# A transformer block on one core: WQ loaded ahead of the second quarter of x, normalisation on ACT, low parts on GpSimd, and one visit of six units per projection

## The chip, the core and the metric

The kernel runs on one core of a Trainium2 chip. A core has five engines that run side by side, each through its own list of instructions in order: TensorE (PE, matrix multiplication, with its weight loads listed as PEld), VectorE (DVE), ScalarE (ACT), GpSimd (POOL) and SyncE (SP), which here issues all DMA transfers. They wait for each other through semaphores only. The metric is the device time of one execution in microseconds. Before the change it is 1258.13 us (median of three runs, 1256.53 to 1259.32).

## The reference

One block of a transformer, with S = 2048 rows of width D = 448, H = 16 heads of width 28 that share one key and one value projection, and a gated feed-forward part of width 1792, all in float32:

```python
def _A_ref(x, wq, wk, wv, wo):
    q = (x @ wq).reshape(B, S, H, Dh).transpose(0, 2, 1, 3)
    k = x @ wk
    v = x @ wv
    scores = jnp.einsum("bhqd,bkd->bhqk", q, k) * (Dh ** -0.5)
    p = softmax(scores, axis=-1)
    o = jnp.einsum("bhqk,bkd->bhqd", p, v)
    return o.transpose(0, 2, 1, 3).reshape(B, S, H * Dh) @ wo
...
h = x + _A_ref(layernorm(x), wq, wk, wv, wo)
return h + (silu(layernorm(h) @ w1) * (layernorm(h) @ w3)) @ w2
```

## The kernel before

**Numbers in two parts.** Most products are made of two rounded halves: a value is split into a high part (an ACT copy into the type float32r) and a low part (the value less its high part), and a product is high by high, low by high and high by low. `mm_D` (L120 to L131) does that for the width 448: eleven matmuls into one PSUM bank, and after the sixth of them it calls `between()` if one is given.

**Quarters.** The 2048 rows are four quarters t = 0 to 3 of 512 columns. For each quarter the program, in the part this change touches, does five things. `stats(t)` takes mean and variance of the four row blocks on DVE (L155, L156), and the inverse root on GpSimd (L161). `norm(t)` makes the four normalised blocks `xn` (L166, DVE) and copies 64 columns of each to its end (L168, GpSimd). `tr(t)` transposes them on PE in four groups c (L179), each into a bank; ACT takes the high part `xh` (L180), and the low part `xl` is a subtraction, on DVE straight from the bank (L187, L189), or, with `spare`, on GpSimd from a copy `rb` that ACT makes of the bank (L184). Of `rb` there are two buffers. `kv(t)` is one `mm_D` for keys and values: ACT writes the high part of the keys (L422), DVE the low part (L423), ACT the values (L425), and then SP copies the 64 rows of the keys to the other 64 partitions (L426) and, when that copy has landed, puts four rows of ones in (L427). `q(t, g)` is one `mm_D` for four heads, taken out by ACT (L446; the first one, and later ones by `build_qs`, go on to the tile QS, by eight DMAs each, L213).

**Units.** Softmax needs the maximum of each row of scores before the exponentials. A `Unit` is one matmul of 128 queries by one quarter kt of the keys (L231, on 64 of the 128 rows of the array) and one maximum over its 512 columns on DVE (L236); `both` is two of them, for the two halves of the array. In the first stage 40 `both`, 80 units, are worked off: 64 of the first group of heads (kt = 0 first, then 1, 2, 3), the maximum over them (L248), and 16 of the second group, with the transposed maxima sent to QS between them (L253 to L267). The list is `first`, and `pairs(n)` takes n `both` from its front. They are mixed with the projections: called as `between` inside an `mm_D` two `both` are taken, and one more by a `pairs(1)` between two projections. They begin when two quarters are through and the third is transposed.

**Banks.** There are seven PSUM banks, given out in the order in which they were released. Every unit, projection and transposed group takes one. So a unit waits for whatever last used its bank: a maximum on DVE, an ACT copy, a DVE copy.

**After that** the main stage begins: for each of 16 groups of heads and 16 key blocks, matmuls (L280), exponentials (L286) and the product with the values (L293), with the units of later groups between them, and then the feed-forward part. Neither is changed, apart from two small GpSimd instructions in each later call of `ln_rstd`.

The order is written out by hand in the program. The loads at the start stand on SP's list in the order first quarter of x, wk, wv, second quarter of x, wq, third, fourth.

Of the kernel before, what the change touches and what calls it, by code (L numbers as in the profile page):

```python
# [16 lines left out]
P = 128  # L17
# [18 lines left out]
def block_kernel(  # L36
# [112 lines left out]
    def ln_stats(t, n):  # L149
        if n == 0:  # L150
            LN[t] = (ln_pool.tile([P, NQ, 6], F32, name="st"),
                     ln_pool.tile([P, NQ, 2], F32, name="mv"),
                     ln_pool.tile([P, NQ], F32, name="rs"), {})
        st, mv, _, _ = LN[t]
        ve.bn_stats(st[:, n], X[t][:, n])  # L155
        ve.bn_aggr(mv[:, n], st[:, n])  # L156

    def ln_rstd(t, n0=0, n1=NQ):
        _, mv, rs, _ = LN[t]
        ve.tensor_scalar(rs[:, n0:n1], mv[:, n0:n1, 1], EPS, None, op0=ALU.add)  # L160
        ge.tensor_tensor(rs[:, n0:n1], rs[:, n0:n1], pexp[:, n0:n1], op=ALU.pow)  # L161

    def ln_norm(t, n):
        _, mv, rs, xns = LN[t]
        xn = xns[n] = ln_pool.tile([P, 512], F32, name="xn", bufs=4)
        ve.tensor_scalar(xn[:, :D], X[t][:, n], mv[:, n, 0:1], rs[:, n : n + 1],  # L166
                         op0=ALU.subtract, op1=ALU.mult)
# [196 lines left out]
    with tc.tile_pool(name="start", bufs=1) as sp:  # L364
# [10 lines left out]
        for m0, w in ((0, wk), (64, wv)):  # L375
            load_w(wkv_r[:, :, m0 : m0 + DH], w)
        sy.dma_start(X[1], xv[1])
        load_w(wq_r, wq)
# [31 lines left out]
        def norm(t):  # L410
            for n in range(NQ):
                ln_norm(t, n)

        def tr(t, *cs):
            for c in cs or range(4):
                ln_tr(t, c)

        def kv(t, between=None):
# [9 lines left out]
            done(ps)  # L428
            return vt

# [24 lines left out]
        def pairs(n=2):  # L455
            while n > 0 and first:
                fn, *args = first.pop(0)
# [275 lines left out]
```

## Time and profile before

| what | us |
|---|---|
| median of three runs | 1258.13 |
| the profiled execution, its own time | 1257.51 |
| its span in the trace | 1255.7 |
| first stage, to the first matmul of L280 | 99.07 |
| main stage, to the first matmul of the feed-forward part | 715.73 |
| feed-forward part | 440.90 |
| PE busy over the span | 1235.7 |
| DVE busy over the span | 860.8 |
| ACT busy over the span | 660.9 |
| POOL busy over the span | 324.3 |

The 1.8 us between the span and the profiled execution's time lie around the traced span. A row of the timeline has the start, the time until the end of the last of its instructions, the engine, the line, the operation, what it writes and reads, the count, and in brackets how long the engine had been idle and what released it. A row of the windows has a window's bounds and length and then, for each engine, busy time and (in brackets) instructions, the granted clock of PE as a share of full speed, and the DMA engines' share and rate. A row of the groups has the count, the busy time, the mean duration of one and the idle time ahead of it.

### The profile page before, as it was taken

How to read it: one execution, taken by the hardware profiler on the slowest of the kernel's cores; microseconds unless marked ns; L12 is line 12 of the kernel's file. 1: busy time of each engine (PE TensorE's matmuls, PEld its weight loads, DVE VectorE, ACT ScalarE, POOL GpSimd, SP SyncE). 2: the span in 40 equal slices, each digit the busy share in tenths (PEclk: the TensorE clock that was granted, in tenths of full speed). 3: DMA queues.
4: the chain of work that ended last, by engine and by line, in shares of the span. 5: the costliest groups of instructions: out<-in, count | busy, mean ns of one | idle time of the engine just before them, and what ended most of it. 6: DMA issues, size and time to landing. Idle time of an engine off the chain costs nothing.

```text
span 1255.7 us, 19960 instructions
## 1 busy us (share of the span) xinstructions
PE 1235.7 (98%) x7596; PEld 768.0 (61%) x7596; DVE 860.8 (69%) x1480; ACT 660.9 (53%) x1255; POOL 324.3 (26%) x240
## 2 busy tenths in 40 slices
PE   6999999999999999999999999999999999999998
PEld 4655444444544444544445543488888888888887
DVE  7998999999898999899998894033333334333333
ACT  3316878887688887688886687921111111211111
POOL 3201011101112101111110110344555445455551
PEclk9999999999999999999999999999999999999999
DMA  6220113110103110112110110023000000000000
GB/s 188 62 45 2 36 32 77 44 25 21 44 2 77 44 40 6 43 24 56 43 45 2 43 28 17 10 79 111 1 30 1 1 1 30 1 1 31 1 1 30
DMA packets 37960, 43.08 MB, mean 34 GB/s; under 512 B 12056, under 2 KB 30680, under 8 KB 37864
## 3 DMA queue, kind: packets, MB, share of 16 engines
q1 hardware_dynamic: 37864, 41.81, 12.8%
q8 instruction: 60, 0.98, 0.3%
q14 instruction: 36, 0.29, 0.1%
HBM read 20.25 MB, written 3.80 MB: 19 GB/s over the span
## 4 chain that ended last, share of the span: by engine, by line
PE 91%; DVE 6%; issue 1%; DMA 1%; POOL 0%; SPq 0%; ACT 0%; POOLq 0%
PE pa L127 23%; PE pb L280 21%; PE po L293 19%; PE pb L641 11%; PE pa L231 9%; DVE mx L236 5%; PE pb L127 4%; PE pa L330 3%; PE pb L179 1%; DMA qs<-mr 0%; PE pb L253 0%; DVE xn L166 0%; DVE nm L248 0%; SPq L267 0%; DMA X<-in_A_x_dram 0%
## 5 line engine op out<-in xcount | busy, mean ns | idle before, releaser
L236 DVE TENSOR_REDUCE mx<-pa 128x1 f32<-128x512 f32 x1024 | 635.9, 682 | 36.3 <-PE pa L231 14.8
L286 ACT ACTIVATE pt<-pb 128x512 f32<-128x512 f32 x1024 | 533.9, 601 | 153.9 <-PE pb L280 118.1
L280 PE MATMUL pb<-qs,KS 64*128 64x512 f32 x2048 | 358.2, 403 | 2.0 <-DMA qs<-mr 2.0
L280 PEld LDWEIGHTS pb<-qs,KS 64*128 64x128 f32 x2048 | 227.5, 185 | 159.8 <-DVE mx L236 80.5
L231 PE MATMUL pa<-KS,qs 64*128 64x512 f32 x1024 | 291.7, 441 | 0.9 <-ACT vt L425 0.9
L293 PE MATMUL po<-pt,VA 128*32 128x512 f32 x2048 | 274.4, 606 | 0.0
L127 PE MATMUL pa<-xh,qs 128*128 128x512 f32 x896 | 235.9, 395 | 0.0
L231 PEld LDWEIGHTS pa<-KS,qs 64*128 64x128 f32 x1024 | 133.7, 184 | 130.8 <-DVE mx L236 86.8
L127 PEld LDWEIGHTS pa<-xh,qs 128*128 128x128 f32 x896 | 167.8, 187 | 38.6 <-issue 0.8
L629 DVE TENSOR_TENSOR pt<-pa,pt 128x512 f32<-128x512 f32 x56 | 38.7, 691 | 222.7 <-PE pa L127 222.7
L641 PE MATMUL pb<-qst,pt 128*128 128x448 f32 x672 | 145.8, 367 | 0.0
L627 ACT ACTIVATE pt<-pa 128x512 f32<-128x512 f32 x56 | 33.5, 598 | 197.6 <-PE pa L127 197.5
L641 PEld LDWEIGHTS pb<-qst,pt 128*128 128x128 f32 x672 | 125.7, 188 | 12.5
L632 ACT ACTIVATE pt<-pt 128x512 fp32r<-128x512 f32 x56 | 35.4, 632 | 152.1 <-DVE pt L629 152.1
L202 POOL TENSOR_TENSOR qst<-QR,qst 128x512 fp32r<-128x512 f32 x15 | 19.3, 1285 | 314.7 <-ACT qst L201 314.7
L127 PE MATMUL pa<-xl,qs 128*128 128x512 f32 x336 | 96.4, 395 | 0.0
L293 PEld LDWEIGHTS po<-pt,VA 128*32 128x32 f32 x2048 | 40.9, 108 | 78.6 <-issue 72.0
L340 POOL TENSOR_TENSOR qs<-QR,qs 128x1024 fp32r<-128x1024 f32 x32 | 76.4, 2388 | 16.2 <-DVE qs L339 16.2
L317 POOL TENSOR_TENSOR OT<-OT,rb 128x512 f32<-128x512 f32 x16 | 20.8, 1298 | 201.3 <-PE pb L280 70.7
L127 PEld LDWEIGHTS pa<-xl,qs 128*128 128x128 f32 x336 | 62.9, 187 | 15.5
L633 DVE TENSOR_TENSOR pt<-pt 128x512 fp32r<-128x512 f32 x56 | 40.8, 728 | 39.1 <-ACT pt L632 39.1
L346 POOL TENSOR_TENSOR qst<-w_wo,qst 128x448 fp32r<-128x448 f32 x24 | 35.3, 1469 | 93.9 <-DVE qst L345 93.9
(80 smaller groups left out, 632.2 us busy)
## 6 DMA issues: line engine op xcount, KB each, us to landing
qs<-qst SPq DMA_DIRECT2D x128, 128.0 KB
rb<-sd SPq DMA_DIRECT2D x64, 64.0 KB
QR<-in_B_w_dram SPq DMA_DIRECT2D x16, 192.0 KB
X<-in_A_x_dram SPq DMA_DIRECT2D x3, 896.0 KB
out_dram<-X SPq DMA_DIRECT2D x3, 896.0 KB
qs<-mr SPq DMA_DIRECT2D x128, 2.0 KB
w<-in_B_w_dram SPq DMA_DIRECT2D x8, 192.0 KB
w_wo<-in_B_w_dram SPq DMA_DIRECT2D x6, 224.0 KB
```

Of the source, the lines that this page charges most:

```text
L127: pe.matmul(ps, lhs[b][:, cb, lsl], rhs[a][:, ca, rsl], start=(k == 0), stop=(k == len(terms) - 1),)
L231: pe.matmul(self.ps, QS[i][r, 2 * self.p, n * P : (n + 1) * P], KS[r, kt * T : (kt + 1) * T], start=True, stop=True)
L236: ve.tensor_reduce(MX[self.i][:, c, self.kt : self.kt + 1], self.ps, axis=AX.X, op=ALU.max)
L280: pe.matmul(self.ps, KS[r, c * P : (c + 1) * P], QS[i][r, 2 * p + k], start=(k == 0), stop=(k == 1))
L286: se.activation(f(PT[i, c, p][:, jj]), self.ps, AF.Exp, bias=0.0, scale=SCALE)
L293: pe.matmul(PO[i][32 * j : 32 * j + 32], VA[:, c], f(PT[i, c, j // 2][:, j % 2]), start=(c == 0), stop=(c == NC - 1))
L330: pe.matmul(ps, OS[a][:, g, n * P : (n + 1) * P], WO[b][:, g], start=(k == 0), stop=(k == 11))
L340: ge.tensor_tensor(wl, W13[k], f(wh), op=ALU.subtract)
L629: ve.tensor_tensor(sg, ps[1], sg, op=ALU.mult)
L632: se.activation(h[:, 0], sg, AF.Copy)
L633: ve.tensor_tensor(h[:, 1], sg, f(h[:, 0]), op=ALU.subtract)
L641: pe.matmul(Y[t][n][:, :D], hid[a][:, n * P : (n + 1) * P], w2s[:, b, :D], start=(k == 0 and m == 0), stop=(k == NF - 1 and m == 2))
```

## The change

WQ goes ahead of the second quarter of x on SP. `norm` of quarters 1 to 3 goes from DVE to ACT, as scale times x plus bias, and for that `ln_rstd` makes a bias `nb` with two GpSimd instructions. The low parts of the transposed quarters 1 to 3 go from DVE to GpSimd, with ACT's second copy `rb`. The order is rewritten: the statistics of the second quarter come after the first `kv`, and the units begin inside the fourth projection of the first quarter. Every unit is taken inside an `mm_D`, three `both` at a time, and `pairs(1)` between projections is gone; since the units begin before all keys are there, `pairs` stops where the next unit's quarter of the keys has not been projected yet.

```diff
     def ln_rstd(t, n0=0, n1=NQ):
...
+        if n1 - n0 == NQ:
+            ge.tensor_tensor(nb, mv[:, :, 0], rs, op=ALU.mult)
+            ge.tensor_scalar(nb, nb, -1.0, None, op0=ALU.mult)
...
+        if act:
+            se.activation(xn[:, :D], X[t][:, n], AF.Identity, bias=nb[:, n : n + 1], scale=rs[:, n : n + 1])
+        else:
+            ve.tensor_scalar(xn[:, :D], X[t][:, n], mv[:, n, 0:1], rs[:, n : n + 1],
+                             op0=ALU.subtract, op1=ALU.mult)
...
+        load_w(wq_r, wq)
         sy.dma_start(X[1], xv[1])
-        load_w(wq_r, wq)
...
         def norm(t):
             for n in range(NQ):
-                ln_norm(t, n)
+                ln_norm(t, n, True)
...
-                ln_tr(t, c)
+                ln_tr(t, c, t > 0)
...
-        def pairs(n=2):
+        def pairs(n=3):
             while n > 0 and first:
-                fn, *args = first.pop(0)
+                fn, *args = first[0]
+                if fn is both and args[3] >= keys[0]:
+                    return
+                first.pop(0)
...
-        tr(0, 0, 1)
-        stats(1, 0)
-        tr(0, 2)
-        stats(1, 1)
-        tr(0, 3)
-        stats(1, 2, 3)
+        tr(0)
         split_wq()
         v0 = kv(0)
+        stats(1, 0, 1, 2, 3)
+        q(0, 0)
         norm(1)
-        q(0, 0)
+        q(0, 1)
+        va(0, v0)
+        stats(2, 0, 1, 2, 3)
         tr(1)
-        stats(2, 0, 1, 2, 3)
-        va(0, v0)
-        q(0, 1)
-        v1 = kv(1)
+        q(0, 2)
         norm(2)
+        q(0, 3, pairs)
+        build_qs(1)
+        v1 = kv(1, pairs)
         stats(3, 0, 1, 2, 3)
-        q(0, 2)
-        q(0, 3)
-        build_qs(1)
         tr(2)
+        q(1, 0, pairs)
         va(1, v1)
-        pairs(1)
+        norm(3)
+        q(1, 1, pairs)
         v2 = kv(2, pairs)
-        pairs(1)
-        norm(3)
-        q(1, 0, pairs)
-        pairs(1)
-        q(1, 1, pairs)
-        pairs(1)
+        q(1, 2, pairs)
         va(2, v2)
-        q(1, 2, pairs)
+        q(1, 3, pairs)
         build_qs(2)
-        pairs(1)
-        q(1, 3, pairs)
         tr(3)
-        pairs(1)
+        q(2, 0, pairs)
         v3 = kv(3, pairs)
         load_wo()
-        for t in (2, 3):
-            for g in range(NG):
-                pairs(1)
-                if (t, g) == (2, 1):
-                    va(3, v3)
-                q(t, g, pairs)
+        for t, g in [(2, 1), (2, 2), (2, 3), (3, 0), (3, 1), (3, 2), (3, 3)]:
+            q(t, g, pairs)
+            if (t, g) == (2, 1):
+                va(3, v3)
         pairs(64)
```

In the changed program the lines of these functions stand a few lines further down: units are L237 and L242, the low part of the keys L429, the low parts on GpSimd L193 and L195, the copies of the keys L432 and L433.

**First place: PE from the third quarter's transposes to the end of `q(1, 0)`, changed program.** `ident` and `xn` are a transpose, `xh`, `xl` and `OS` (which holds WQ here) a projection, `KS` and `qs` a unit; a name in brackets is what the instruction waits for.

```order
L185 MATMUL pb<-ident,xn 128x128 [waits DVE_49,Pool_49]
L185 MATMUL pb<-ident,xn 128x128 [waits Pool_49] x3
L127 MATMUL pb<-xh,OS_95 128x512 [waits DVE_49]
L127 MATMUL pb<-xh,OS_95 128x512 x2
L127 MATMUL pb<-xl,OS_95 128x512 x3
L237 MATMUL pa<-KS,qs 128x512 [waits DVE_49]
L237 MATMUL pa<-KS,qs 128x512 [waits Activation_49]
L237 MATMUL pa<-KS,qs 128x512 [waits PE_49,Activation_49] x2
L237 MATMUL pa<-KS,qs 128x512 [waits DMAHW3_49,PE_49,Activation_49]
L237 MATMUL pa<-KS,qs 128x512 [waits DMAHW2_49,PE_49,Activation_49]
L127 MATMUL pb<-xh,OS_96 128x512 x3
```

The same projection on PE in the program before:

```order
L231 MATMUL pa<-KS,qs 128x512 [waits DVE_49] x2
L127 MATMUL pb<-xh,OS_95 128x512 [waits DVE_49]
L127 MATMUL pb<-xh,OS_95 128x512 x2
L127 MATMUL pb<-xl,OS_95 128x512 x3
L231 MATMUL pa<-KS,qs 128x512 [waits DMAHW7_49,DMAHW6_49,DVE_49]
L231 MATMUL pa<-KS,qs 128x512 [waits DMAHW1_49,DMAHW0_49,DVE_49]
L231 MATMUL pa<-KS,qs 128x512 [waits DVE_49]
L231 MATMUL pa<-KS,qs 128x512 [waits Activation_49]
L127 MATMUL pb<-xh,OS_96 128x512 x3
```

Two and four units have become six in one place; the last four of them now use banks that ACT releases with the copies `rb` of the third quarter, and the last two also read the second quarter of the keys (the two DMA waits). In the program before these units stand after quarters 0 to 2 are all through, and wait for DVE.

**Second place: DVE and GpSimd around the fourth quarter's statistics.** DVE in the changed program, from the units of `q(0, 3)` and `kv(1)` on:

```order
L242 TENSOR_REDUCE mx<-pa 128x1 [waits PE_49] x12
L429 TENSOR_TENSOR KS<-pb,KS 32x512 [waits Activation_49]
L155 BN_STATS st<-X_83 128x6 [waits DMAHW7_49]
L156 BN_AGGR mv<-st 128x2 [waits DVE_49,Pool_49]
L155 BN_STATS st<-X_83 128x6
```

Three more such pairs follow, then the line that feeds the inverse root (L160), and only then the next six units. The same stretch of DVE in the program before, from that line on:

```order
L160 TENSOR_SCALAR rs<-mv 128x4 [waits DVE_49]
L187 TENSOR_TENSOR xl<-pb,xh 128x512 [waits Activation_49] x3
L189 TENSOR_TENSOR xh<-pb,xh 64x512 [waits Activation_49]
L435 COPY VA<-pb 128x4x28 [waits PE_49]
L236 TENSOR_REDUCE mx<-pa 128x1 [waits PE_49] x6
```

GpSimd in the changed program, from the tile `qst` of `build_qs(1)` to the end of the third quarter's low parts:

```order
L208 TENSOR_TENSOR qst<-QR_88,qst 128x512 [waits Activation_49]
L161 TENSOR_TENSOR rs<-rs,pexp 128x4 [waits DVE_49]
L163 TENSOR_TENSOR nb<-mv,rs 128x4 [waits Pool_49]
L164 TENSOR_SCALAR nb<-nb 128x4 [waits Pool_49]
L193 TENSOR_TENSOR xl<-rb,xh 128x512 [waits PE_49,Activation_49]
L193 TENSOR_TENSOR xl<-rb,xh 128x512 [waits Activation_49] x2
L195 TENSOR_TENSOR xh<-rb,xh 64x512 [waits PE_49,Activation_49,Pool_49]
```

The statistics of the fourth quarter now stand on DVE behind twelve units and the low part of the keys, and on GpSimd the third quarter's low parts stand behind the inverse root of the fourth. Before, these low parts were DVE's own, ahead of all units.

**Third place: PE at `kv(3)` and `q(2, 1)`.** Changed program, from the start of `kv(3)` (`WKV`):

```order
L127 MATMUL pb<-xh,WKV_113 96x512 [waits DVE_49]
L127 MATMUL pb<-xh,WKV_113 96x512 x2
L127 MATMUL pb<-xl,WKV_113 96x512 [waits Pool_49] x3
L127 MATMUL pb<-xh,WKV_114 96x512 x3
L127 MATMUL pb<-xh,WKV_113 96x512 [waits Pool_49]
L127 MATMUL pb<-xh,WKV_114 96x512
L127 MATMUL pb<-xh,OS_95 128x512 [waits DVE_49]
L127 MATMUL pb<-xh,OS_95 128x512 x2
L127 MATMUL pb<-xl,OS_95 128x512 x3
L237 MATMUL pa<-KS,qs 128x512 [waits DMAHW7_49,DVE_49]
L237 MATMUL pa<-KS,qs 128x512 [waits DMAHW6_49]
L237 MATMUL pa<-KS,qs 128x512 x3
```

There is no unit inside `kv(3)` any more, and the next unit, in `q(2, 1)`, waits for the two DMAs that complete the keys of `kv(3)` itself. In the program before, the first unit that reads these keys stands after three more projections:

```order
L127 MATMUL pb<-xh,OS_95 128x512 [waits DVE_49]
L127 MATMUL pb<-xh,OS_95 128x512 x2
L127 MATMUL pb<-xl,OS_95 128x512 x3
L231 MATMUL pa<-KS,qs 128x512 [waits DVE_49] x2
L231 MATMUL pa<-KS,qs 128x512 [waits Activation_49]
L231 MATMUL pa<-KS,qs 128x512 [waits DVE_49]
L127 MATMUL pb<-xh,OS_96 128x512 x3
L127 MATMUL pb<-xh,OS_95 128x512
L127 MATMUL pb<-xh,OS_96 128x512
L231 MATMUL pa<-KS,qs 128x512 [waits DMAHW7_49,DVE_49]
L231 MATMUL pa<-KS,qs 128x512 [waits DMAHW6_49,DVE_49]
```

More of the change, by code (lines that the diff above doesn't have):

```diff
@@ L152, in ln_stats @@
                      ln_pool.tile([P, NQ, 2], F32, name="mv"),
-                     ln_pool.tile([P, NQ], F32, name="rs"), {})
-        st, mv, _, _ = LN[t]
+                     ln_pool.tile([P, NQ], F32, name="rs"), {}, ln_pool.tile([P, NQ], F32, name="nb"))
+        st, mv, _, _, _ = LN[t]
         ve.bn_stats(st[:, n], X[t][:, n])
@@ L158, in ln_rstd, with ln_norm @@
     def ln_rstd(t, n0=0, n1=NQ):
-        _, mv, rs, _ = LN[t]
+        _, mv, rs, _, nb = LN[t]
         ve.tensor_scalar(rs[:, n0:n1], mv[:, n0:n1, 1], EPS, None, op0=ALU.add)
         ge.tensor_tensor(rs[:, n0:n1], rs[:, n0:n1], pexp[:, n0:n1], op=ALU.pow)
-    def ln_norm(t, n):
-        _, mv, rs, xns = LN[t]
-        xn = xns[n] = ln_pool.tile([P, 512], F32, name="xn", bufs=4)
-        ve.tensor_scalar(xn[:, :D], X[t][:, n], mv[:, n, 0:1], rs[:, n : n + 1],
-                         op0=ALU.subtract, op1=ALU.mult)
+        if n1 - n0 == NQ:
+            ge.tensor_tensor(nb, mv[:, :, 0], rs, op=ALU.mult)
+            ge.tensor_scalar(nb, nb, -1.0, None, op0=ALU.mult)
+    def ln_norm(t, n, act=False):
+        _, mv, rs, xns, nb = LN[t]
+        xn = xns[n] = ln_pool.tile([P, 512], F32, name="xn", bufs=4)
+        if act:
[3 more added lines that the diff above has]
+                             op0=ALU.subtract, op1=ALU.mult)
         ge.tensor_copy(xn[:, D:], xn[:, 384:D])
@@ L428, in kv @@
             done(ps)
+            keys[0] += 1
             return vt
+        keys = [0]
         def va(t, vt):
```

## The prediction

> **What bounds the kernel now.** I read the windows first. After the start PE has hardly an idle moment in the first stage, and DVE is nearly full too:
>
> ```profile
> 22.40:39.40 17.00, 17.00 (x93) 13.59 (x91) 14.29 (x33) 8.11 (x15) 4.69 (x7) 0.97 0.32 71
> 39.40:99.07 59.67, 57.95 (x253) 35.10 (x253) 55.84 (x96) 11.67 (x21) 4.22 (x6) 1.00 0.25 54
> ```
>
> From 39.4 to 99.07 us PE works 57.95 and DVE 55.84 of 59.67; ACT (11.67) and POOL (4.22) have room. The groups of this stretch, then the timeline of one projection with its six units, then one row of the chain of work, tell which of the two limits:
>
> ```profile
> L236 DVE TENSOR_REDUCE mx<-pa 128x1 f32<-128x512 f32 x80 | 49.1, 680 | 2.5 <-PE pa L231 2.3
> ...
> 73.28 0.73 PE L231 MATMUL pa<-KS,qs 64*128 64x512 f32 x4
> 73.82 3.68 DVE L236 TENSOR_REDUCE mx<-pa 128x1 f32<-128x512 f32 x6 [0.30 <-PE pa L231]
> 73.94 1.42 PE L127 MATMUL pb<-xh,OS 128*128 128x512 f32 x5
> 75.30 0.50 PE L231 MATMUL pa<-KS,qs 64*128 64x512 f32 x2
> 75.72 0.96 PE L127 MATMUL pb<-xh,OS 128*128 128x512 f32 x3
> 77.31 0.74 PE L231 MATMUL pa<-KS,qs 64*128 64x512 f32 x4
> ...
> 25.17 10.28 PE pb L127 x44
> ```
>
> The last row is four projections in a row: 10.28 / 44 = 0.234 a matmul, 2.57 a projection. With six units it takes 77.31 - 73.28 = 4.03, from start to start 0.66, 1.36, 0.42 and 1.59. Five and six matmuls alone would be 1.17 and 1.40, and two units take about 0.22, so each of the four changes between units and projection costs about 0.2. PE is the longer by a little: DVE needs 3.68 (0.613 a maximum) and then waits 0.3 for PE.
>
> **The change part by part.** Times are on the clock of the profiled execution, 1257.51 us with a span of 1255.7; the median of three is 1258.13, 0.6 more. What counts is when the main stage begins: it keeps its order, so a shift there is a shift of the end.
>
> ```profile
> 99.07 0.97 PE L280 MATMUL pb<-qs,KS 64*128 64x512 f32 x5
> ```
>
> *The start.*
>
> ```profile
> 13.43 1.98 ACT L390 ACTIVATE OS<-OT 128x448 fp32r<-128x448 f32 x4 [0.32 <-DMA OT<-in_A_wq_dram]
> 16.81 1.33 POOL L161 TENSOR_TENSOR rs<-rs,pexp 128x4 f32<-128x4 f32 x1 [5.66 <-DVE rs L160]
> 18.11 2.36 POOL L392 TENSOR_TENSOR OS<-OT,OS 128x448 fp32r<-128x448 f32 x2
> 19.29 0.50 PE L127 MATMUL pb<-xh,OS 128*128 128x512 f32 x1 [2.25 <-POOL OS L392]
> 20.52 2.08 PE L127 MATMUL pb<-xh,OS 128*128 128x512 f32 x4 [0.74 <-POOL OS L392]
> 22.40 2.41 PE L179 MATMUL pb<-ident,xn 128*128 128x128 f32 x16
> 22.64 0.60 ACT L204 ACTIVATE qst<-pb 128x512 fp32r<-128x512 f32 x1 [3.50 <-PE pb L127]
> ...
> 1.25 0.10 POOL L362 MEMSET pexp<- 128x4 f32 x1
> ```
>
> Loading WQ earlier is worth ACT's 0.32 by itself. The rest comes from the order: POOL's split of WQ stood behind the inverse root of the second quarter. Now it can begin when ACT has split the first of four parts, 13.7, and ends at 16.1 (2.36). The first projection then ends at 17.3 instead of 22.6, and the second at 19.6. By then DVE does the second quarter's statistics (16.6 to 19.8), then POOL the inverse root and `nb` (21.6), ACT the four `xn` (1.98 as in L390, 23.65): PE waits about 3 us, and the second quarter's transposes end near 25.4, where they ended at 24.8. The gain of 5.3 is gone; what is left of it is that two projections and not one are done.
>
> The two `nb` instructions are in no row: nearest are a 128x4 memset, 0.10, and the 128x4 power, 1.01 to 1.33; I take 0.3 each, nearer the cheap one as it is plain arithmetic. Nor is an ACT copy with scale and bias from memory: I take L390's 0.5, and 0.65 (`rb` below) as the upper end, 0.6 for four; the lower end is DVE's time, no worse. [...]
>
> *Units begin earlier.* POOL's low parts of the second quarter (1.29 each) free `rb` so that ACT's last `rb` ends at 28.95; PE does `q(0,2)` and half of `q(0,3)` by 29.4. So the first maximum is at 30.0, and was here:
>
> ```profile
> 39.95 3.67 DVE L236 TENSOR_REDUCE mx<-pa 128x1 f32<-128x512 f32 x6
> ```
>
> From there DVE has 49.1 for the 80 maxima, 3.2 for the fourth quarter's statistics, 2.1 for three low parts of keys, 1.3 for small copies: 55.7; the transposes' low parts and the normalisation have left it. A projection with six units in one place costs PE two changes less, 4.03 - 0.41 = 3.62, about DVE's 3.68. With no wait at all, DVE would be through at 85.7, and 3.5 of projection would follow: main stage at 89.2, 9.9 us earlier. That is the whole gain. Now the waits.
>
> *Wait 1, in `q(1,0)`.*
>
> ```profile
> 33.52 0.62 DVE L155 BATCH_NORM_STATS2 st<-X 128x6 f32<-128x448 f32 x1
> ...
> 36.57 0.17 DVE L160 TENSOR_SCALAR rs<-mv 128x4 f32<-128x4 f32 x1
> ...
> 36.82 1.01 POOL L161 TENSOR_TENSOR rs<-rs,pexp 128x4 f32<-128x4 f32 x1 [2.85 <-DVE rs L160]
> ...
> L184 ACT ACTIVATE rb<-pb x8: 645/646/648, 372.3 to 574.9; 128x512 f32<-128x512 f32 x8
> ...
> L187 POOL TENSOR_TENSOR xl<-rb,xh x6: 1292/1292/1300, 373.0 to 569.7; 128x512 fp32r<-128x512 f32 x6
> ```
>
> Statistics take 36.74 - 33.52 = 3.2. Twelve maxima (30.05 to 37.55, as PE brings the second six at once) stand ahead of the keys' low part (to 38.25) and these statistics (to 41.45); then the power (42.5) and `nb` (43.1). Only then POOL does the third quarter's low parts, 1.29 each, to 44.4 and 45.7. ACT's third and fourth `rb` wait for those two buffers: 45.1 and 46.4. Units 17 and 18 of the list use their banks. PE has done `kv(1)`, the transposes and half of `q(1,0)` by 39.1 and is held, in order, from 41.2 to 46.45 but for one unit. Behind it stand the second half of `q(1,0)`, `va(1)` and half of `q(1,1)`, 1.36 + 0.4 + 1.6, before DVE, which ran dry at 43.9 but for two maxima, gets the next six: 50.75.
>
> *Waits 2 and 4, for the copies of the keys.*
>
> ```profile
> 18.55 0.51 SPq L426 DMA_DIRECT2D KS<-KS  x1
> 21.05 0.65 SPq L427 DMA_DIRECT2D KS<-ones  x1
> ...
> 41.95 0.59 ACT L422 ACTIVATE KS<-pb 64x512 fp32r<-64x512 f32 x1 [3.40 <-PE pb L127]
> 43.65 0.68 DVE L423 TENSOR_TENSOR KS<-pb,KS 32x512 fp32r<-32x512 f32 x1
> 44.36 0.50 SPq L426 DMA_DIRECT2D KS<-KS  x1
> 46.61 0.54 SPq L427 DMA_DIRECT2D KS<-ones  x1
> ```
>
> The second issue comes 2.25 after the first, when that copy has landed. No row shows the ones landing: I take 2.25 for them too, as the same kind of transfer (bounds: 0.54, their issue alone, and 2.5, as at the first pair above). So keys are readable 4.5 us after the low part. Before, nothing read keys so fresh. Now twelve maxima run from 50.75 to 58.1, the low part of `kv(2)` ends at 58.8, keys at 63.3; PE gets to the third unit of `q(1,2)` at 58.1 and waits **5.2**, with `va(2)` and `q(1,3)` behind it, whose units come at 67.3. *Wait 3* is wait 1 again, smaller, in `q(2,0)`: `build_qs(2)` stands ahead of the fourth quarter's copies on ACT and POOL, and the last two units wait for `rb` until 75.5 (2.2). The rest of `q(2,0)` and `kv(3)` end at 79.6, ACT and DVE take 0.7 each, keys at 85.5; PE has half of `q(2,1)` to do until 81.0 and waits **4.5**.
>
> *To the end.* Units of `q(2,1)` at 85.5, of `q(2,2)` at 89.9; from 90.4 DVE has 26 maxima and 0.5 of small things, until 106.9; PE issues the last two units at 105.5, then half of `q(3,2)` and `q(3,3)`, 1.36 + 2.57: main stage at 109.65, **10.6 later**.
>
> *PE's clock.*
>
> ```profile
> 18.00:19.00 1.00, 0.00 (x0) 0.00 (x0) 0.97 (x2) 0.45 (x1) 1.00 (x2) 1.00 0.00 0
> 20.00:21.00 1.00, 0.47 (x1) 0.48 (x2) 1.00 (x2) 0.00 (x0) 0.96 (x3) 0.51 0.33 68
> 22.00:23.00 1.00, 1.00 (x5) 0.80 (x4) 0.00 (x0) 0.36 (x1) 0.00 (x0) 0.50 0.03 8
> 23.00:24.00 1.00, 1.00 (x10) 1.00 (x9) 0.69 (x1) 0.74 (x3) 0.00 (x0) 0.79 0.00 0
> ```
>
> After an idle gap of 2.25 us the granted clock was half from 20.0 to about 23.4, of which PE worked 2.9: 1.4 lost. Waits 1, 2 and 4 are longer gaps, and behind each of them DVE waits for PE: 3 x 1.4 = **4.2** (bounds 0 and 3 x 1.7, the full 3.4 at half). [...]
>
> Hidden: ACT's 24 new copies and POOL's 12 low parts, but where named, in the room shown at the top; the later `nb`, in the main stage's POOL. Sum: 1257.5 + 10.6 + 4.2 = **1272.3**.
>
> **The rivals.**
> - *The waits, but the clock stays up*: the few units within the gaps count as work. 1257.5 + 10.6 = 1268.1. For it: one gap is all the evidence. Chance 0.20.
> - *Only the keys' waits are real*: the third and fourth quarters' low parts come in time. Without waits 1 and 3 (5.0 and 2.2), with two slow clocks: 10.6 - 7.2 + 2.8 = 6.2, 1263.7. Against it: the order on POOL. Chance 0.10.
> - *Faster.* The earlier first maximum decides, if DVE, full to 55.84 of 59.67 now, goes through its 55.7 without gaps: 1257.5 - 9.9 = 1247.6. From there to 1268.1 are 20.5 us of waits and refilling; if less than 9.9 of them are paid, the change wins. Against it: each wait stands in the order itself. Chance 0.08.
> - *No change*: about half of the 20.5 is paid, 1257.5. Chance 0.04.
> - *The load doesn't bring the start forward*: the second quarter of x, now behind WQ, arrives after 16.6. The DMA engines were idle from about 17.5 with everything loaded (0.00 in the row of 18 to 19), so at most 1 us more, inside the forecast's bounds.
>
> **How the numbers follow.** The forecast has the remaining 0.58; its own bounds are 1269 (ones landing at once, twice 1.7 less) to 1277 (`nb` at 1.0 each, the slow clock at 1.7). The range leaves out the two last cases with a time of their own, 0.12, and a little at the top: 1261 to 1278. Faster by over 0.2% 0.08, within 0.2% (about what a measurement of this kernel can tell from no change) 0.04, slower 0.88.
>
> **What would show it.** Right: the first projection's `qst` near 17.3, the first maximum near 30; PE idle for 3 to 5 us inside `q(1,0)`, released by ACT's `rb`, and inside `q(1,2)` and `q(2,1)`, released by the ones; granted clock near 0.5 behind them; main stage between 110 and 115. Wrong: DVE full from 30 us on, keys readable after 2 us, or full clock behind the gaps.

## The result and the profile after

| kernel | median, us | runs, us | ratio to before, 95% interval | span of the profiled run | main stage begins |
|---|---|---|---|---|---|
| before | 1258.04 | 4 runs, 1256.53 to 1259.32 | 1 | 1255.7 | 99.07 |
| after | 1280.76 | 4 runs, 1278.30 to 1280.87 | 1.0177 [1.0162, 1.0192] | 1276.4 | 119.72 |

The changed kernel is slower by 1.8%. The forecast was 1272.3 with a range from 1261 to 1278: the direction is right, the size too small, and the time lies above the range. The profiled execution is the fastest of the four (1278.30). Lines behind the edited functions have moved by six: the units are now L237, the maxima L242, the first matmul of the main stage L286.

The timeline's row of the main stage, and a row of the windows for the stretch from the first maximum to the main stage (length; then busy time and instructions of PE, PEld, DVE, ACT and POOL; the granted clock), of the kernel before and of the changed one, and the changed kernel's group of maxima in that stretch:

```profile
119.72 0.96 PE L286 MATMUL pb<-qs,KS 64*128 64x512 f32 x5
...
39.95:99.07 59.12, 57.40 (x252) 34.75 (x251) 55.32 (x95) 11.67 (x21) 4.22 (x6) 1.00 0.25 55
...
33.80:119.72 85.92, 70.10 (x294) 45.82 (x291) 55.48 (x97) 24.50 (x44) 17.22 (x21) 0.88 0.18 39
...
L242 DVE TENSOR_REDUCE mx<-pa 128x1 f32<-128x512 f32 x80 | 49.3, 681 | 29.4 <-PE pa L237 29.3
```

The main stage begins 119.72 - 99.07 = 20.65 later, and the span is 20.7 longer: everything happened ahead of it, as the prediction had it. VectorE's work in the stretch is the forecast's (55.48; forecast 55.7) and the stretch starts 6.15 earlier, but it takes 85.92 in the place of 59.12. For 29.3 us of it VectorE stands in front of maxima and waits for TensorE, and TensorE's granted clock is 0.88 on average.

The start, in the timeline of the changed kernel, with the row of before for the split of WQ on VectorE:

```profile
16.64 1.16 DVE L392 TENSOR_TENSOR OS<-OT,OS 128x448 fp32r<-128x448 f32 x2
...
13.72 2.65 POOL L398 TENSOR_TENSOR OS<-OT,OS 128x448 fp32r<-128x448 f32 x2 [2.50 <-ACT OS L396]
14.61 2.25 DVE L398 TENSOR_TENSOR OS<-OT,OS 128x448 fp32r<-128x448 f32 x2 [0.71 <-ACT OS L396]
18.22 0.60 ACT L210 ACTIVATE qst<-pb 128x512 fp32r<-128x512 f32 x1
22.57 2.71 ACT L170 ACTIVATE xn<-X,nb,rs 128x448 f32<-128x448 f32 x4 [3.75 <-POOL nb L164]
25.33 3.03 PE L185 MATMUL pb<-ident,xn 128*128 128x128 f32 x13 [0.18 <-ACT xn L170]
33.80 7.35 DVE L242 TENSOR_REDUCE mx<-pa 128x1 f32<-128x512 f32 x12 [8.86 <-PE pa L237]
```

VectorE's two instructions took 1.16 before, while POOL ran only the small power of L161, and take 2.25 now that POOL's two run at the same time. `qst` is at 18.22 in the place of 17.3, the first maximum at 33.80 in the place of 30.0. Windows of 2 us show what TensorE's clock did behind its wait for `xn`:

```profile
22.00:24.00 2.00, 0.33 (x1) 0.14 (x1) 1.90 (x7) 1.44 (x3) 0.67 (x3) 0.94 0.59 131
24.00:26.00 2.00, 1.62 (x5) 1.03 (x6) 0.88 (x3) 1.92 (x4) 1.14 (x4) 0.50 0.86 197
26.00:28.00 2.00, 2.00 (x12) 2.00 (x11) 0.00 (x0) 2.00 (x5) 1.83 (x4) 0.50 0.90 201
28.00:30.00 2.00, 2.00 (x7) 1.61 (x6) 0.00 (x0) 1.79 (x4) 2.00 (x3) 0.50 0.00 0
30.00:32.00 2.00, 2.00 (x9) 1.65 (x8) 0.00 (x0) 0.29 (x1) 1.92 (x2) 0.85 0.04 8
```

At half from about 23.8 to 30.6: 6.8 us. The missing share of each window, doubled, gives that length: 2 x 2 x (0.06 + 0.5 + 0.5 + 0.5 + 0.15) = 6.8.

The four waits in the timeline, with the keys' low part and the issue of the ones ahead of wait 2 and the next six units behind waits 2 and 4, and then the windows behind wait 2:

```profile
48.81 0.79 PE L237 MATMUL pa<-KS,qs 64*128 64x512 f32 x1 [3.69 <-ACT rb L190]
50.03 0.79 PE L237 MATMUL pa<-KS,qs 64*128 64x512 f32 x1 [0.43 <-ACT rb L190]
...
63.55 0.68 DVE L429 TENSOR_TENSOR KS<-pb,KS 32x512 fp32r<-32x512 f32 x1
...
66.52 0.54 SPq L433 DMA_DIRECT2D KS<-ones  x1
68.47 1.22 PE L237 MATMUL pa<-KS,qs 64*128 64x512 f32 x4 [4.93 <-DMA KS<-ones]
...
75.27 0.97 PE L237 MATMUL pa<-KS,qs 64*128 64x512 f32 x6
...
82.15 0.50 PE L237 MATMUL pa<-KS,qs 64*128 64x512 f32 x1 [0.78 <-ACT rb L190]
83.38 0.50 PE L237 MATMUL pa<-KS,qs 64*128 64x512 f32 x1 [0.73 <-ACT rb L190]
...
93.34 1.65 PE L237 MATMUL pa<-KS,qs 64*128 64x512 f32 x6 [4.17 <-DMA KS<-ones]
...
99.91 0.96 PE L237 MATMUL pa<-KS,qs 64*128 64x512 f32 x6
```

```profile
66.00:68.00 2.00, 0.00 (x0) 0.00 (x0) 0.00 (x0) 0.00 (x0) 0.00 (x0) 1.00 0.03 8
68.00:70.00 2.00, 1.53 (x5) 0.91 (x6) 0.73 (x2) 0.00 (x0) 0.00 (x0) 0.53 0.04 8
70.00:72.00 2.00, 2.00 (x5) 1.11 (x4) 1.75 (x3) 0.00 (x0) 0.00 (x0) 0.50 0.00 0
72.00:74.00 2.00, 2.00 (x8) 1.66 (x8) 0.28 (x1) 0.60 (x1) 0.00 (x0) 0.50 0.00 0
74.00:76.00 2.00, 2.00 (x10) 1.15 (x8) 0.20 (x1) 0.00 (x0) 0.00 (x0) 0.76 0.00 0
```

All four waits are where the prediction put them and end on what it named: `rb` in `q(1,0)` and `q(2,0)`, the ones of KS in `q(1,2)` and `q(2,1)`. Behind wait 2 the clock falls at about 68.1, just ahead of TensorE's new start, and it stays at half for 6.8 us, with TensorE busy: 2 x 2 x (0.47 + 0.5 + 0.5 + 0.24) = 6.8. At waits 1 and 4 it falls while TensorE still waits (at 47.7 and 92.0), again for 6.8 us each. The next six units come at 75.27, 6.8 us behind the wait in the place of the 4.0 that the forecast had at full clock. Behind wait 4 it is 99.91 - 93.34 = 6.6 in the place of 4.4.

### The profile page after: what moved, and what is told of

It is laid out like the page before. It is cut to its first block, busy times and chain, and to the rows that moved or that the text cites. A ratio compares the mean times of both kernels' runs of the same rounds, so it can differ in the third digit from the quotient of the medians.

```text
span 1276.4 us, 20000 instructions
## 1 busy us (share of the span) xinstructions
PE 1242.3 (97%) x7596; PEld 775.3 (61%) x7596; DVE 847.0 (66%) x1456; ACT 674.9 (53%) x1279; POOL 342.9 (27%) x266
## 4 chain that ended last, share of the span: by engine, by line
PE 90%; DVE 7%; DMA 1%; POOL 1%; ACT 0%; issue 0%; SPq 0%; POOLq 0%; DVEq 0%
PE pa L127 22%; PE pb L286 22%; PE po L299 19%; PE pb L642 11%; PE pa L237 8%; DVE mx L242 5%; PE pb L127 3%; PE pa L336 3%; PE pb L185 1%; DVE st L155 1%; POOL xl L193 0%; DMA KS<-KS 0%; PE pb L259 0%; DMA KS<-ones 0%; DMA qs<-mr 0%
## 5 line engine op out<-in xcount | busy, mean ns | idle before, releaser
L242 DVE TENSOR_REDUCE mx<-pa 128x1 f32<-128x512 f32 x1024 | 636.1, 682 | 64.3 <-PE pa L237 44.2
L286 PE MATMUL pb<-qs,KS 64*128 64x512 f32 x2048 | 358.1, 403 | 1.8 <-DMA qs<-mr 1.8
L286 PEld LDWEIGHTS pb<-qs,KS 64*128 64x128 f32 x2048 | 227.1, 185 | 158.8 <-DVE mx L242 81.2
L237 PE MATMUL pa<-KS,qs 64*128 64x512 f32 x1024 | 291.1, 441 | 15.8 <-DMA KS<-ones 9.1
L237 PEld LDWEIGHTS pa<-KS,qs 64*128 64x128 f32 x1024 | 134.4, 185 | 145.2 <-DVE mx L242 84.5
L323 POOL TENSOR_TENSOR OT<-OT,rb 128x512 f32<-128x512 f32 x16 | 20.7, 1291 | 198.3 <-DMA rb<-sd 83.4
```

What stands on the lines that cost most here:

```text
L237: pe.matmul(self.ps, QS[i][r, 2 * self.p, n * P : (n + 1) * P], KS[r, kt * T : (kt + 1) * T], start=True, stop=True)
L242: ve.tensor_reduce(MX[self.i][:, c, self.kt : self.kt + 1], self.ps, axis=AX.X, op=ALU.max)
L286: pe.matmul(self.ps, KS[r, c * P : (c + 1) * P], QS[i][r, 2 * p + k], start=(k == 0), stop=(k == 1))
```

## Experiments

Theory: the loss is the four waits, and behind each the half clock, whose price the prediction took too small. Rivals: VectorE's maxima set the end whatever TensorE does; single parts of the change (load, normalisation, low parts, six units) cost by themselves. Twelve kernels ran. A difference to the changed kernel is that of the two ratios times 1258; two ratios each known to about 0.0015 give such a difference to some 2.6 us.

| run | median, us | ratio, 95% interval | to after, us |
|---|---|---|---|
| keys later | 1267.90 | 1.0072 [1.0058, 1.0086] | -13.2 |
| gaps filled | 1274.47 | 1.0128 [1.0114, 1.0141] | -6.2 |
| statistics later | 1277.01 | 1.0146 [1.0132, 1.0160] | -3.9 |
| six units alone, from before | 1255.88 | 0.9984 [0.9975, 0.9993] | |
| four buffers | 1274.30 | 1.0134 [1.0119, 1.0149] | -5.4 |
| start filled | 1277.92 | 1.0164 [1.0148, 1.0179] | -1.6 |
| low parts on VectorE | 1273.23 | 1.0124 [1.0107, 1.0141] | -6.7 |
| normalisation on VectorE | 1279.51 | 1.0177 [1.0162, 1.0192] | 0.0 |
| x ahead of WQ | 1278.71 | 1.0158 [1.0145, 1.0171] | -2.4 |
| all waits | 1261.11 | 1.0021 [1.0011, 1.0030] | -19.6 |
| start and six, from before | 1255.41 | 0.9981 [0.9972, 0.9990] | |
| gaps half filled | 1276.22 | 1.0147 [1.0130, 1.0164] | -3.8 |

**Keys later.** The keys of the third and fourth quarter are read one projection later.

```diff
-        keys = [0]
+        keys, ready = [0], [0]
...
             done(ps)
+            ready[0] = keys[0]
...
-                if fn is both and args[3] >= keys[0]:
+                if fn is both and args[3] >= (keys[0] if args[3] < 2 else ready[0]):
```

(`ready` is set at the end of `q`.)

> The changed kernel, but the keys of the third and fourth quarter are read by the first maxima only from the visit after the next Q projection on, not in the projection that follows their own (the work is the same, in another order; the visit in q(1,2) holds one pair instead of three, and the one in q(2,1) none). Theory of the prediction: the time was lost where TensorE stood for the fresh keys in q(1,2) and q(2,1), 4.9 and 4.2 us of waiting by the changed kernel's trace, and behind each the clock stood at half, 2.8 and 2.2 us. Then both waits and both slow stretches go: 11 to 14 us faster than the changed kernel, 1267 to 1270. Rival 1, the clock has another cause and stays low there: 8 to 9 us, 1272. Rival 2, the waits only stand in front of a bound by VectorE's maxima, which move but don't shrink: under 4 us, 1277 to 1281.

Measured -13.2 us, as expected. The two waits shrink, in the timeline, to

```profile
68.48 1.05 PE L237 MATMUL pa<-KS,qs 64*128 64x512 f32 x6 [1.54 <-DMA KS<-ones]
...
87.80 0.96 PE L237 MATMUL pa<-KS,qs 64*128 64x512 f32 x6 [1.38 <-DMA KS<-ones]
```

and behind both the clock stays at 1. The main stage begins at 108.91. Two waits and what follows them are more than half of the loss; a bound by VectorE is ruled out here, as its work didn't change.

**Gaps filled.** The waits stay, but TensorE has work in them that nothing reads. This parts wait and clock.

```diff
+        def idle_work(n, x):
...
+            for _ in range(n):
+                pe.matmul(po, w[:, 0], x[:, 0], start=True, stop=True)
...
+                if fn is both and args[0] == 0 and (args[1], args[2], args[3]) in ((0, 0, 2), (0, 0, 3)):
+                    idle_work(*((18, XT[1][0]) if args[3] == 2 else (15, XT[2][0])))
```

> The changed kernel with work added that nothing reads: 18 matmuls of 512 columns ahead of the first units on the third quarter's keys, 15 ahead of those on the fourth's, into a bank that is free there (about 4.2 and 3.5 us at 0.234 us each, inside the waits of 4.9 and 4.2 us). The waits' ends don't move. Theory of the prediction, where a wait also costs the half clock behind it: the units and projections behind run at full clock, 2.8 + 2.2 us by the changed kernel's trace, so 4 to 5 us faster than the changed kernel, 1276, with the granted clock near 1 there. Rival, the low clock behind the waits has another cause: no gain (0 to 1 us slower), 1281, with the clock still at 0.5.

Measured -6.2 us, and 4.1 between the two profiled spans (1272.3 beside 1276.4). The added matmuls (L468) and the units behind them in the timeline, then the same places in windows:

```profile
64.39 4.37 PE L468 MATMUL po<-xh,OS 128*128 128x512 f32 x18
69.40 0.72 PE L237 MATMUL pa<-KS,qs 64*128 64x512 f32 x4 [0.64 <-DMA KS<-ones]
```

```profile
68.00:70.00 2.00, 1.36 (x8) 0.63 (x6) 0.09 (x1) 0.00 (x0) 0.00 (x0) 1.00 0.01 4
70.00:72.00 2.00, 2.00 (x12) 1.41 (x11) 2.00 (x4) 0.48 (x1) 0.00 (x0) 1.00 0.04 8
```

The keys come no sooner, TensorE does 33 matmuls more, and the kernel is faster. The next units come at 73.36, 4.0 behind the wait, exactly the forecast's distance at full clock; behind wait 4 it is 4.2 in the place of 6.6. That saves 2.8 and 2.4 us; 1.0 of it is lost again behind wait 1, where the clock in this execution is at half for 10.2 us and not 6.8, and so the spans differ by 4.1. The half clock behind waits 2 and 4 thus costs 4 to 6 us by itself; the prediction had 2 x 1.4 = 2.8, at most 3.4.

**Gaps half filled.** The same with 9 and 7 matmuls, which leaves gaps of 2.64 and 2.59.

```diff
-                    idle_work(*((18, XT[1][0]) if args[3] == 2 else (15, XT[2][0])))
+                    idle_work(*((9, XT[1][0]) if args[3] == 2 else (7, XT[2][0])))
```

> The run with the two gaps filled, but with 9 and 7 added matmuls in the place of 18 and 15 (2.1 and 1.6 us of the waits of 4.9 and 4.2; nothing reads them), so that gaps of 2.8 and 2.6 us are left. The traces show the half clock in stretches of one, two or three times 3.4 us at fixed places, whatever ended the wait. Theory, what counts is how much of such a stretch TensorE worked: gaps of 2.6 to 2.8 fall into one stretch in some executions and are divided between two in others, so that the clock falls behind some of them and for a shorter time: a third to two thirds of what the full filling gave (1.0128 against 1.0177), 1.0140 to 1.0165, with executions that differ by more than 1 us. [...] Rival 2, any gap over 2 us costs the full price: 1.0170 and more.

Measured -3.8, between the two. In one execution, two gaps of nearly one length end differently:

```profile
68.51 1.22 PE L237 MATMUL pa<-KS,qs 64*128 64x512 f32 x4 [2.64 <-DMA KS<-ones]
...
93.39 0.96 PE L237 MATMUL pa<-KS,qs 64*128 64x512 f32 x6 [2.59 <-DMA KS<-ones]
```

The same places in windows that are steps of 3.41 us, counted from the 68.14 at which the clock falls:

```profile
64.73:68.14 3.41, 1.14 (x5) 0.59 (x4) 0.86 (x2) 0.16 (x1) 0.00 (x0) 1.00 0.18 41
68.14:71.55 3.41, 3.04 (x9) 2.02 (x9) 2.25 (x4) 0.00 (x0) 0.00 (x0) 0.50 0.02 5
71.55:74.97 3.42, 3.42 (x12) 2.32 (x10) 0.51 (x2) 0.60 (x1) 0.00 (x0) 0.50 0.00 0
...
88.62:92.03 3.41, 2.19 (x10) 1.47 (x8) 0.55 (x1) 0.59 (x1) 0.00 (x0) 1.00 0.17 38
92.03:95.45 3.42, 2.06 (x11) 1.40 (x11) 1.55 (x3) 0.00 (x0) 0.00 (x0) 1.00 0.61 136
```

Behind the first the clock is at half for 6.8 us, behind the second not at all. The length of the gap alone didn't decide here: 2.3 us of the first lie in one step, in which TensorE worked only 1.14, while the second is divided between two, with 2.19 and 2.06 of work. This is the theory's "how much of such a stretch TensorE worked". The four executions differ by 3.1 us (1275.79 to 1278.90). Rival 2 falls on the full clock behind the second gap.

**Start filled.** Nine matmuls ahead of the first transpose of the second quarter, one ahead of each of the next three.

```diff
+    def idle_work(n):
...
+            if (t, c) == (1, 0):
+                idle_work(1 if n else 9)
             pe.transpose(ps[:, n * P : (n + 1) * P], xns[n][:, c * P : (c + 1) * P], ident)
```

> The changed kernel with 12 matmuls of 512 columns added that nothing reads, at the start: nine ahead of the first transpose of the second quarter (TensorE stands 2.4 us there), and one ahead of each of the next three. Theory: the half clock of that stretch (0.50 from 24 to 30 us in the changed kernel's trace) comes from that gap; filled, the clock stays at 1, the transposes and q(0,2) behind take about 1.9 + 0.9 instead of 3.0 + 1.6, and the first maximum comes 1 to 2 us before the 33.8 of the changed kernel, the time 1 to 2 us below its 1280.8. This would be the part of the start that the prediction left out. Rival, the stretch has another cause, or what is won at the start is lost in the wait behind it (wait 1 has its end from GpSimd and the statistics, not from TensorE): 0 to 0.5 us.

The first maximum comes 2.5 us earlier and the clock is at 1 there:

```profile
31.33 1.89 DVE L250 TENSOR_REDUCE mx<-pa 128x1 f32<-128x512 f32 x3 [6.39 <-PE pa L245]
```

But the main stage begins only 0.4 earlier in the profiled execution (119.30), and the runs give -1.6, no more than they can resolve. The windows around wait 2, which here ends at 67.09:

```profile
64.00:66.00 2.00, 0.00 (x0) 0.00 (x0) 0.18 (x1) 0.00 (x0) 0.00 (x0) 0.69 0.30 66
66.00:68.00 2.00, 0.91 (x4) 0.53 (x4) 0.11 (x1) 0.00 (x0) 0.00 (x0) 0.50 0.01 4
68.00:70.00 2.00, 2.00 (x6) 1.47 (x5) 2.00 (x4) 0.00 (x0) 0.00 (x0) 0.50 0.03 8
70.00:72.00 2.00, 2.00 (x8) 1.19 (x8) 0.65 (x2) 0.60 (x1) 0.00 (x0) 0.50 0.00 0
72.00:74.00 2.00, 2.00 (x6) 1.15 (x4) 0.00 (x0) 0.00 (x0) 0.00 (x0) 0.50 0.00 0
74.00:76.00 2.00, 2.00 (x10) 1.36 (x10) 1.08 (x2) 0.00 (x0) 0.00 (x0) 0.75 0.00 0
```

Half for 2 x 2 x (0.31 + 4 x 0.5 + 0.25) = 10.2 us now, three times 3.4 and not twice: the wait came earlier, the return of the clock did not. Behind wait 1 it is 10.2 us in this execution, too. Of the 2.5 us won at the start, 1.0 is lost behind wait 1, 0.6 behind wait 2 and 0.4 behind wait 4. That filling the gap keeps the clock up at the start is shown; for the time, the theory's 1 to 2 us and the rival's 0 to 0.5 both lie within what the runs can resolve.

**Statistics later and four buffers**, the two edits on wait 1.

```diff
-        stats(3, 0, 1, 2, 3)
         tr(2)
         q(1, 0, pairs)
+        stats(3, 0, 1, 2, 3)
```

> The changed kernel with the statistics of the fourth quarter moved behind q(1,0), so that GpSimd's low parts of the second... third quarter's x no longer stand behind them. Theory of the prediction: wait 1, two units held until 48.8 and 50.0 us for banks that ScalarE's copy holds for GpSimd's low part, was made by that queue; then the last of them runs about 2 to 3.5 us earlier, and the half clock behind it (1.7 us) shrinks with it: 2 to 4 us faster than the changed kernel, 1277 to 1279. Rival, the banks are held by GpSimd's own three low parts at 1.2 us each whatever stands ahead, or the gain is taken back by the later normalisation of the fourth quarter: 0 to 1 us.

```diff
-            x32 = wk_pool.tile([P, T], F32, name="rb")
+            x32 = (start_pool[0].tile([P, T], F32, name="x32", bufs=4) if start_pool
+                   else wk_pool.tile([P, T], F32, name="rb"))
```

> The changed kernel, with four buffers of their own for ScalarE's copies ahead of GpSimd's low parts in the place of two shared ones. The copies, and so the banks, then no longer wait for GpSimd. Theory: the trace of the changed kernel shows TensorE waiting 6.7 us in all for banks behind that copy (wait 1 in q(1,0), 3.7 the longest, and wait 3 in q(2,0), 1.5); the queue on GpSimd makes them through the two buffers. The run with the statistics later showed that the keys of the second quarter stand right behind: there the first units on them waited 2.3 us for the keys and went at 46.8 instead of 48.8. So wait 1 shrinks by 2 to 3 and not to nothing, and wait 3 goes (1.5): with some slow clock saved 4 to 6 us faster than the changed kernel (1280.8), 1275 to 1277. Rival 1, the buffers are all there is to wait 1: 8 us and more, 1272 or less. Rival 2, the low parts are then late for the projections that read them: under 2 us.

Measured -3.9 and -5.4, both as the theory had it. Either edit takes the long hold on the banks (3.69 and 0.43) away, two short ones of 0.6 and 0.5 stay, and the same second wait appears (the row is that of four buffers; with the statistics later it reads 46.78 and 2.31):

```profile
46.71 0.89 PE L238 MATMUL pa<-KS,qs 64*128 64x512 f32 x2 [2.31 <-DMA KS<-ones]
```

Units 17 and 18 are the first on the second quarter's keys. The prediction saw the queue on POOL and not that these units stand for fresh keys too, 2 us earlier: without wait 1 there is still a wait.

**Low parts and normalisation on VectorE again**, one part of the change undone at a time.

```diff
-                ln_tr(t, c, t > 0)
+                ln_tr(t, c)
```

> The changed kernel with one part undone: the low parts of x's second to fourth quarter on VectorE again, straight out of PSUM, without ScalarE's copy. Theory of the prediction: the waits for banks (1 and 3, 6.7 us in the trace) come from this part. Undone, they go, though keys of the second quarter still are a wait in q(1,0); VectorE gets 3 x 4 x 0.69 = 8.3 us of work, but it stands idle for 33 us in front of late maxima, so that most of it fits: 2 to 6 us faster than the changed kernel (1280.8), 1275 to 1279. Rival, VectorE's maxima are what sets the end, and its 8.3 us more are simply added: 5 to 8 us slower, 1286 to 1289.

```diff
-                ln_norm(t, n, True)
+                ln_norm(t, n)
```

> The changed kernel with another part undone: the normalisation of the second to fourth quarter on VectorE again (the small tile of mean times power stays computed, and nothing reads it). Theory of the prediction as mended by the trace: ScalarE's four take 2.7 us and wait for two more small operations on GpSimd (0.6 with their gaps), VectorE's four take 4 x 0.51 = 2.0, so the first maximum comes about 1.3 us earlier; later quarters are not on the path, and their 2.0 us each fit into VectorE's idle time: 1 to 2 us faster than the changed kernel (1280.8), 1279 to 1280. Rival, VectorE is where the stage is bound, and the 6 us of work come on top: 3 to 6 us slower, 1284 to 1287.

Without GpSimd's low parts it is -6.7 us, no more above the 2 to 6 expected than the runs can resolve: VectorE's 8.3 us of added work fit into its idle time. Wait 1 is then 2.94 for VectorE's own low part and 0.41 for the keys, at 46.24 and 47.75. Without the normalisation on ScalarE the time doesn't change by anything the runs can resolve. The first maximum comes 1.9 earlier (31.91), but the units behind it are held by `rb` (0.99 and 0.89), VectorE is busy with the next normalisation in front of its maxima (one of its four instructions took 1.46 beside GpSimd's low parts; in the kernel before the median of L166 is 0.51), and the half clock moves to 32 us (0.53 from 32 to 34, 0.50 from 34 to 36). Neither the theory's 1 to 2 us nor the rival's loss is seen.

**x ahead of WQ**, the order of the two loads undone.

```diff
-        load_w(wq_r, wq)
         sy.dma_start(X[1], xv[1])
+        load_w(wq_r, wq)
```

> The changed kernel with the order of two loads undone: the second quarter of x ahead of WQ, as before. Theory of the prediction: the earlier load is worth 0.3 us at the start (before, the split of WQ waited 0.32 us for WQ), and that is hidden or lost further on: 0 to 0.5 us slower than the changed kernel (1.0177 of before). Rival 1, the load is what brings the first projection forward: 2 us and more slower. Rival 2, x's second quarter lands earlier and its statistics start sooner: faster by up to 1 us.

In the trace the split of WQ starts 0.47 later (14.19 on POOL) and the first maximum 0.53 later (34.33): the size of the prediction's 0.32. The time is -2.4 us, with intervals that overlap; the profiled execution has 1279.17 beside 1278.30. Nothing shows that the earlier load gains anything, and whether it loses 1 or 2 us was not settled.

**All waits.** Keys of every quarter read a projection later (`args[3] >= ready[0]`), the four buffers and the filled start together.

> The changed kernel with all the waits that the prediction named taken away at once: keys of every quarter are read only after the projection that follows theirs, four buffers for ScalarE's copies, and the 12 added matmuls at the start that nothing reads. Theory: waits and the slow clock behind them are the whole of the loss. Alone these edits gave 12.9, 5.4 and 1.6 us; with the second quarter's keys' wait (2.3 and some 1.7 of slow clock) added it is 20 to 25 us: 0.995 to 1.001 of before, 1252 to 1259 beside 1258, and the main stage begins at 95 to 99 us. Rival, a further cost of the change stands behind them (VectorE's maxima, 46 pairs by 2 by 0.613 us is 56.4, can't end before 31.3 + 56.4, but smaller waits add up): the sum falls short, 1.004 and more.

Measured -19.6 of the 22.3 that the change costs, just short of what was expected: the ratio is above the theory's 1.001 and below the rival's 1.004. The timeline's row and the windows' row from its first maximum:

```profile
100.04 0.96 PE L295 MATMUL pb<-qs,KS 64*128 64x512 f32 x5
...
31.34:100.04 68.70, 63.75 (x294) 42.22 (x291) 55.15 (x97) 24.11 (x44) 18.14 (x23) 0.98 0.22 49
```

Waits and clock are nearly all of the loss. Still TensorE idles 5 us and VectorE 13.5 in this stretch: two waits of 1.4 for keys remain, four short ones for banks behind transposes, and a visit without ripe units is a hole for VectorE. The no-wait case of the prediction, a main stage at 89.2, was not reached. Twelve timed executions of this kernel show without any edit that the time goes with the clock: two with a mean granted clock of 1.000 took 1258.31, three with 0.997 took 1260.93 to 1261.17, two with 0.994 took 1263.53 and 1263.72.

**Six units alone; with the start's order.** Both start from the kernel before.

```diff
-        def pairs(n=2):
+        def pairs(n=3):
...
-        pairs(1)
...
```

(The other six calls `pairs(1)` go as well.)

> The kernel before, with one edit of the change alone: one visit of six units per projection in the place of two of four and two (the start, the normalisation, the low parts and the keys' conditions stay as they were). Theory of the prediction: a projection that holds one visit takes 3.62 instead of 4.03 us, and the visits don't reach fresh keys where TensorE would wait; some 11 projections by 0.41 is 4.5 us faster than before, 1253 to 1254. Rival 1, VectorE's maxima at 3.68 us a visit set the pace in both: no change, 1258. Rival 2, the larger visits reach the third quarter's keys early here too, and the waits of the changed kernel come with them: 5 to 10 us slower, 1263 to 1268.

```diff
-        sy.dma_start(X[1], xv[1])
         load_w(wq_r, wq)
+        sy.dma_start(X[1], xv[1])
...
         split_wq()
         v0 = kv(0)
+        stats(1, 0, 1, 2, 3)
+        q(0, 0)
         norm(1)
-        q(0, 0)
+        q(0, 1)
+        va(0, v0)
         tr(1)
         stats(2, 0, 1, 2, 3)
-        va(0, v0)
-        q(0, 1)
         v1 = kv(1)
```

> The kernel before with two parts of the change: six units in one visit, as in the run of that part alone (0.9984), and the order of the start (WQ ahead of the second quarter of x, the statistics of that quarter behind the first keys, the second Q projection ahead of its transposes). Normalisation, low parts and the place of the first visit stay as before. Theory of the prediction: the start's order frees WQ's split and is worth up to 2 us of TensorE ahead of the first maximum (40 us in the run of six units alone), which carries through to the end as no wait for keys is near: 0.9968 to 0.9984, 1254 to 1256. Rival 1, it carries nothing, since VectorE's transposed low parts and statistics in front of the first maximum set it: 0.998 to 0.999. Rival 2, the normalisation now comes later and the wait moves to the transposes: 1.000 and more.

Six units in one visit are 2 us faster than before (0.9984), half of the 4.5 expected; in the profiled execution the main stage begins 0.7 earlier (98.40). From its first maximum VectorE is busy 54.99 of 57.90:

```profile
40.50:98.40 57.90, 55.73 (x251) 35.59 (x248) 54.99 (x94) 11.70 (x21) 4.21 (x6) 1.00 0.25 56
```

That VectorE's 3.68 a visit cuts TensorE's 0.41 per projection short is read from this row; TensorE is as full, and no run parts the two. With the start's order it is 0.9981, the same. That lies in the theory's range and in rival 1's; the first maximum, at 40.21 beside 40.45, speaks for rival 1. These two are the fastest of all and beat both kernels, the one before by not quite 0.2%.

## Why the prediction was wrong

- **What bounds the kernel** and where it counts: right. The shift of the main stage is the shift of the end, VectorE's work was as forecast, and the visits take 3.6 and 3.8 (units at 99.91, 103.52, 107.34; forecast 3.62). From the units of `q(2,2)` to the main stage it is 19.8 (forecast 19.75).
- **Waits 1 to 4**: right in place, releaser and order; 4.93 and 4.17 for the keys (forecast 5.2 and 4.5, as the ones landed somewhat sooner than the 2.25 taken), 1.5 for wait 3 (forecast 2.2). What it missed about wait 1 is the second cause behind the first.
- **The clock, "3 x 1.4 = 4.2 ... (bounds 0 and 3 x 1.7, the full 3.4 at half)": this step failed.** It took the one example of before, one stretch of 3.4 us at half, as the price of a gap and as its bound. Every gap of over 2 us from 10 us on in the changed kernel's profiled execution (2.39, 3.69, 4.93 and 4.17) is followed by two such stretches, 6.8 us; in other runs it was one (2.25, before), two (4.92, four buffers), three (3.69, keys later) or none (2.59, gaps half filled). In the changed kernel TensorE is only partly busy in the first of the two each time (1.83 to 3.08 of 3.41) and full in the second. Filling two of the gaps gave 6.2 us where the step had 2.8 and at most 3.4.
- **The start**: mis-sized by 3.8, the first maximum at 33.80 for 30.0, and this is the same failure in part. 1.0 is the later start of the four `xn` (22.57 for 21.6), behind the statistics of the second quarter; some 0.6 of it, by estimate, is VectorE's half of WQ's split, slowed beside POOL's (at 1.16 the low part of the keys could have followed at 16.23, when ACT had made the high part, and not at 16.89). 0.73 is the four `xn` themselves (2.71 for 1.98); the other 2.1 follow on half clock over the second quarter's transposes and `q(0,2)`. The prediction saw a gap of "about 3 us" there and did not price it as a gap. The row of L390 that was taken for the four copies was too low.
- In one sum, on the clock of the profiled execution: the main stage was forecast at 109.65 + 4.2 = 113.85 and came at 119.72, 5.9 later. Up to the end of wait 1 (50.03, forecast 46.45) 3.6 of it are there; behind waits 1, 2 and 4 the clock took 1.9 + 2.8 + 2.2 = 6.9 where 4.2 were counted, 2.7 more; all the rest together gives 0.4 back. The other 2.5 between 1278.3 and the median go with a lower clock too (0.985 to 0.987 beside 0.988); those executions have no trace, so where it was low is open.
- **Six units**: 0.41 a projection on TensorE was right for TensorE, but in the kernel before it is worth 2 us and not 4.5. **The rival "faster"** rested on paying less than 9.9 of 20.5 us of waits; with all named waits gone the kernel still only comes near to the time before. "The clock stays up" and "only the keys' waits" are ruled out by the 0.50 behind the waits and by wait 1's 3.69.

## What to carry to other kernels

A new wait on TensorE cost its length here and then, mostly, the half clock on what followed: two, at worst three times 3.4 us at half. Put that into the range for every gap like those here (2.25 to 4.93 us), the one at the start (2.39) too, and add up short waits that stand close together (0.46 and 0.49 with four buffers had 3.4 us at half behind them). Work handed to an idle engine was not free here, as buffers on the critical path waited in that engine's queue: the low parts back on VectorE gave 6.7 us, four buffers 5.4. Read what was just written by DMA one stage later (13.2 us here), and if the wait can't go, matmuls whose result nothing reads can pay for themselves (6.2 us here).

## What the runs showed of the hardware

- The granted clock was at half in stretches of 3.4, 6.8 and 10.2 us, which are one, two and three steps of 3.41. In the changed kernel's profiled execution they begin at 23.76, 47.66, 68.14 and 92.02, and these are 7, 6 and 7 such steps apart. In eight of the profiled executions (both kernels, keys later, gaps filled, four buffers, start filled, all waits, start and six), between 10 and 110 us, every step with 1.45 us of work on TensorE or less was followed by one at half, and no step at full clock with over 2.46; from 1.86 to 2.46 there are both. So in these runs a gap cost by its place among the steps: 2.64 us cost two of them and 2.59 none within one execution, and with four buffers two waits of 0.46 and 0.49 us in one step (2.46 of work) cost one. A gap of 2.31 us had 6.8 us at half there, from 45.9 on. What brings the clock back stays open: 2.90 us of work in a step at half was enough before, 3.08 behind wait 2 was not.
- Two 128x448 subtractions on VectorE took 1.16 us beside a 128x4 power on GpSimd and 2.25 beside two of the same kind there. GpSimd's own two took 2.65 beside them, and 2.36 before, beside VectorE's normalisation.
- Keys were readable 4.2 us after VectorE's low part (63.55 + 0.68 to 68.47): 2.3 until the second, dependent issue, 1.95 for its landing.
